# Low halves of two output-weight chunks formed by TensorE and ScalarE instead of TensorE and VectorE, with a new order of all instructions

## The chip, the cores and the metric

One core of one Trainium2 chip. The metric is the device time of one execution in microseconds (us), lower is better. The kernel before took 509.13 us (median of 3 runs, 508.42 to 509.32). One more execution was profiled: it took 508.1 us, and its first to last instruction span 506.3 us.

Engines are named as in the profile: PE is TensorE (PEld its weight loads), DVE is VectorE, ACT is ScalarE, POOL is GpSimd, SP is SyncE, which issues the DMAs.

## What is computed

Banded attention over 8 batches x 8 heads x 576 tokens x 64, then a gated MLP. Inputs q, k, v come as float32, the weights as float64.

```python
scores = where(mask, q @ k.T / 8, -1e9)          # heads 0-3: last 32 keys; heads 4-7: every 32nd key
x = (softmax(scores) @ v) as (B, S, 512)
h = maximum(x @ w_in, 0)                          # w_in 512 x 1024
conv[s] = cw[0]*h[s-1] + cw[1]*h[s] + cw[2]*h[s+1]
out = (h * sigmoid(conv)) @ w_out                 # w_out 1024 x 512
```

## The kernel before, in words

**Split numbers.** The big products keep float32 accuracy with TensorE's faster fp32r type. Each operand is kept as a high half (the value rounded to fp32r) and a low half (what is left), and a product is three fp32r matmuls: high x high, low x high, high x low. `mm1` (L622) makes x @ w_in that way from `wih`, `wil`, `xh`, `xl` (L633); `mm2` (L707) makes the output from `woh`, `wol`, `gh`, `gl` (L721).

**Groups.** The 4608 tokens are worked in 9 groups of 512. A group's `mm1` makes eight 128-row tiles f = 0 to 7; `conv_gate` (L642) takes each through ReLU out of PSUM (ACT, L650), the middle tap (ACT L681, or DVE L684 for some tiles of group 0), two more taps (DVE L690), sigmoid (ACT L694), the gate product (L698, on DVE or POOL) and the split into `gh` (ACT L388) and `gl` (L391, on DVE or POOL). Then `mm2` makes four output tiles. The attention of the next batch (L431 scores, L538 times v, and the softmax between on DVE and ACT) is woven in.

**Weights.** `convert` (L298) takes a chunk of weights from its float64 words: |high word| (ACT L281), a clamp (L283), four integer and float steps on DVE (L285 to L291) that leave a float32 `t` in the word buffer `ws` and a remainder `tail` in `wl`; then ACT rounds `t` to the high half (L355). The low half is t + tail - high. There are eight chunks c = 0 to 7: four of w_in, then w_out's wo0 to wo3 (c = 4 to 7); each low half is made in two pieces. A letter of `SPLIT_W` (L44, by c) says how:

```python
if how == "a":
    def whole(ps=ps, b=b):
        nc.tensor.matmul(ps, eye, half(t, b), start=True, stop=False)      # L368
        nc.tensor.matmul(ps, eyer, half(tail, b), start=False, stop=False) # L369
        nc.tensor.matmul(ps, negr, block(wh, b), start=False, stop=True)   # L370
    ...
    op(A, 0.59, ..., nc.scalar.copy(block(wlo, b), four(ps)))              # L372
else:
    def less(ps=ps, b=b):
        nc.tensor.matmul(ps, eyer, half(tail, b), start=True, stop=False)  # L375
        nc.tensor.matmul(ps, negr, block(wh, b), start=False, stop=True)   # L376
    ...
    op(V, 0.69, ..., nc.vector.tensor_tensor(out=block(wlo, b), in0=four(half(t, b)), in1=four(ps), op=ALU.add))  # L378
```

`eye` is a float32 identity and `t` is float32, so L368 is a full float32 matmul; `eyer` and `negr` are fp32r identities, one of them negated.

**Order.** Every instruction is recorded as an operation with a number (`Plan.op`), and `emit` (L185) issues them in the sequence of the table `ORDER` (L55). Each engine runs its own instructions in that order and waits where an operand or buffer isn't ready. `FILLS` (L139) puts warm-up matmuls (`busy`, L742) that compute nothing ahead of an operation: 9: (18, 1, 18) means 18 of them ahead of operation 9, into PSUM bank 1, the first 18 of them 512 columns wide, the others 256. Bank -1 is the first half of the attention's PSUM tile `r`. The other tables choose engines by letter, p for POOL, v for DVE, a for ACT: `CLAMP` (L283, by chunk), `GATE` and `FIRST_GATE` (L698), `SPLIT_G` and `FIRST_SPLIT_G` (L391), `FIRST_SCALE` (L681 or L684 in group 0).

## Time and profile before

| | |
|---|---|
| median of 3 runs | 509.13 us |
| profiled execution, its time / its span | 508.1 us / 506.3 us |
| PE busy | 495.9 us (98%), 6997 matmuls |
| PE weight loads busy | 401.9 us (79%) |
| DVE busy | 364.8 us (72%) |
| ACT busy | 337.1 us (67%) |
| POOL busy | 138.3 us (27%) |
| DMA | 51.45 MB, mean 102 GB/s |
| warm-up matmuls (L742) | 105 |

Matmuls are pipelined, so the duration of one matmul in a row overlaps the next; what a matmul costs the stream is the distance from its start to the next start. A row of the timeline says how long the engine was idle before it, and what ended that wait.

### The profile page before, as it was taken

The numbers are of one execution on the slowest core, as the hardware profiler recorded it, in microseconds if no ns is written. First come the engines' busy times: TensorE is split into PE (matmuls) and PEld (weight loads), VectorE is DVE, ScalarE is ACT, GpSimd is POOL, SyncE is SP. The second block draws the span as 40 slices with busy tenths as digits, with TensorE's granted clock in tenths as the row PEclk, the third lists the DMA queues.
The fourth block names the chain that finished last, engine by engine and source line by source line (L and its number), as shares of the span: only waits on it lengthen the run. The fifth ranks groups of instructions, "written<-read, shape, count | busy, mean of one in ns | idle before, by whom it ended". The sixth has DMA issues, their size and how long they took to land.

```text
span 506.3 us, 16055 instructions
## 1 busy us (share of the span) xinstructions
PE 495.9 (98%) x6997; PEld 401.9 (79%) x6997; DVE 364.8 (72%) x640; ACT 337.1 (67%) x653; POOL 138.3 (27%) x225
## 2 busy tenths in 40 slices
PE   8899999999999999999999999999999999999997
PEld 4476778887888888887888888888888888888797
DVE  3999998658976786777939896777688846643740
ACT  3877988558846785578648964875588647635741
POOL 1201323223310534055204220414014521442610
PEclk9999999999999999999999999999999999999999
DMA  8776603152142331314151223601442010002002
GB/s 299 286 247 217 241 2 113 66 179 82 34 129 85 112 128 50 138 60 155 38 172 42 65 97 128 197 22 61 131 157 71 1 62 23 1 0 84 0 2 85
DMA packets 17351, 51.45 MB, mean 102 GB/s; under 512 B 2048, under 2 KB 2944, under 8 KB 17280
## 3 DMA queue, kind: packets, MB, share of 16 engines
q1 hardware_dynamic: 17280, 50.41, 29.0%
q8 instruction: 55, 0.90, 0.8%
q14 instruction: 16, 0.13, 0.1%
HBM read 40.97 MB, written 9.44 MB: 100 GB/s over the span
## 4 chain that ended last, share of the span: by engine, by line
PE 77%; ACT 6%; DVE 5%; issue 1%; DMA 1%; POOL 1%; ACTq 0%; DVEq 0%; POOLq 0%
PE m L721 37%; PE m L633 30%; PE r L538 5%; PE r L431 4%; DVE misc L690 2%; ACT misc L681 1%; DMA ws<-in_dram 1%; ACT misc L694 1%; ACT misc L650 1%; ACT gh L388 1%; DVE gl L391 1%; ACT t L467 1%; POOL gl L391 0%; ACT wa L281 0%; DVE misc L698 0%
## 5 line engine op out<-in xcount | busy, mean ns | idle before, releaser
L690 DVE SCALAR_TENSOR_TENSOR misc<-misc,cw 128x512 f32<-128x512 f32 (+25 forms) x256 | 129.3, 549 | 32.4 <-ACT misc L681 31.9
L721 PE MATMUL m<-gh,woh 128*128 128x512 f32 (+2 forms) x320 | 119.9, 375 | 0.7 <-ACT misc L650 0.6
L721 PE MATMUL m<-gl,woh 128*128 128x512 f32 (+2 forms) x320 | 118.0, 369 | 0.2 <-DVE gl L391 0.2
L721 PE MATMUL m<-gh,wol 128*128 128x512 f32 (+2 forms) x320 | 117.8, 368 | 0.0
L633 PE MATMUL m<-xh,wih 128*128 128x512 f32 x288 | 114.1, 396 | 0.0
L633 PE MATMUL m<-xl,wih 128*128 128x512 f32 x288 | 112.4, 390 | 0.2 <-ACT xl L594 0.2
L633 PE MATMUL m<-xh,wil 128*128 128x512 f32 x288 | 112.3, 390 | 0.0
L698 POOL TENSOR_TENSOR misc<-misc 128x512 f32<-128x512 f32 (+1 forms) x40 | 46.4, 1164 | 114.8 <-ACT misc L694 113.9
L721 PEld LDWEIGHTS m<-gh,woh 128*128 128x128 f32 x320 | 60.0, 188 | 11.9 <-ACT misc L650 1.6
L721 PEld LDWEIGHTS m<-gl,woh 128*128 128x128 f32 x320 | 60.1, 188 | 10.9 <-DVE gl L391 0.7
L721 PEld LDWEIGHTS m<-gh,wol 128*128 128x128 f32 x320 | 60.1, 188 | 9.6
L681 ACT ACTIVATE misc<-misc,cw 128x383 f32<-128x383 f32 (+12 forms) x125 | 61.3, 526 | 7.3 <-POOL misc L652 2.8
L694 ACT ACTIVATE misc<-misc 128x512 f32<-128x512 f32 (+1 forms) x72 | 45.3, 632 | 29.5 <-DVE misc L690 29.2
L633 PEld LDWEIGHTS m<-xl,wih 128*128 128x128 f32 x288 | 54.1, 188 | 12.2 <-ACT xl L594 0.7
L633 PEld LDWEIGHTS m<-xh,wih 128*128 128x128 f32 x288 | 54.1, 188 | 11.7 <-ACT misc L650 0.2
L633 PEld LDWEIGHTS m<-xh,wil 128*128 128x128 f32 x288 | 54.1, 188 | 10.8
L391 POOL TENSOR_TENSOR gl<-misc,gh 128x512 fp32r<-128x512 f32 (+1 forms) x38 | 48.1, 1266 | 49.9 <-ACT gh L388 43.6
L388 ACT CAST gh<-misc 128x512 fp32r<-128x512 f32 (+1 forms) x72 | 44.1, 618 | 25.8 <-DVE misc L698 13.9
L650 ACT ACTIVATE misc<-m 128x512 f32<-128x512 f32 x72 | 42.2, 593 | 14.5 <-PE m L633 10.4
L728 ACT COPY misc<-m 128x512 f32<-128x512 f32 (+2 forms) x40 | 21.0, 544 | 35.2 <-PE m L721 35.2
L571 ACT CAST xh<-r 128x576 fp32r<-128x576 f32 (+13 forms) x56 | 23.8, 431 | 28.3 <-DVE t L456 12.6
L652 POOL COPY misc<-carry 128x2 f32<-128x2 f32 x64 | 20.3, 330 | 79.0 <-DVE misc L698 47.4
(77 smaller groups left out, 597.3 us busy)
## 6 DMA issues: line engine op xcount, KB each, us to landing
qk<-in_dram SPq DMA_DIRECT2D x32, 592.0 KB, 5.7
v<-in_dram SPq DMA_DIRECT2D x32, 384.0 KB, 4.4
ws<-in_dram SPq DMA_DIRECT2D x14, 512.0 KB, 4.8
out_dram<-misc SPq DMA_DIRECT2D x28, 256.0 KB, 2.9
misc<-in_dram SPq DMA_DIRECT2D x2, 512.0 KB, 5.2
out_dram<-misc SPq DMA_DIRECT2D x4, 255.5 KB, 2.5
out_dram<-misc SPq DMA_DIRECT2D x3, 256.5 KB, 2.1
more<-in_dram SPq DMA_DIRECT2D x1, 320.0 KB, 7.9
```

Of the source, the lines that this page charges most:

```text
L388: op(A, ta, at, lambda: nc.scalar.copy(hi(), src), [skey], [(k, "h") for k in [key] + over])
L391: lambda: eng.tensor_tensor(out=lo(), in0=src, in1=hi().bitcast(F32), op=ALU.subtract),
L538: nc.tensor.matmul(psV[64 * h:64 * h + 64, o:o + n_], v[W * c:W * c + W, h, j], tt[W * c:W * c + W, 64 * NBLK * h + a:64 * NBLK * h + z], ...
L571: op(A, 0.162 + 0.00083 * (z - a), at + offset[8], lambda hi=hi, src=src: nc.scalar.copy(hi, src), ko, [("xh", hp, x) for x in halves])
L633: nc.tensor.matmul(ps, a[:, c, fs], x[:, c, N * x0:N * x0 + N], start=(n == 0 and m == 0), stop=(n == NC - 1 and m == 2))
L650: op(A, 0.596, at + cg[2], lambda: nc.scalar.activation(out=h[:, 2:N + 2], in_=ps, func=AF.Relu), [kp], [("h", hi)])
L681: op(A, 0.17 + 0.00108 * (z - a), at + cg[3], lambda a=a, z=z: nc.scalar.activation(out=c_[:, a:z], in_=h[:, a + 1:z + 1], func=AF.Copy, s ...
L690: op(V, 0.22 + 0.00103 * (z - a), at + cg[4] + 0.4 * k, lambda k=k, wk=wk, a=a, z=z: nc.vector.scalar_tensor_tensor(out=c_[:, a:z], in0=h[ ...
L694: op(A, 0.63, at + cg[5], lambda: nc.scalar.activation(out=c_[:, :n], in_=c_[:, :n], func=AF.Sigmoid), [kc], [kc], table=1)
L698: op(ge, 0.69 if ge == V else 1.28, at + cg[6], lambda: (nc.vector if ge == V else nc.gpsimd).tensor_tensor(out=c_[:, :n], in0=h[:, 1:n + ...
L721: nc.tensor.matmul(ps, a[:, f, ms], row(y, g, f)[:, tok], start=(f == 0 and n == 0), stop=(f == NF - 1 and n == 2))
L728: op(A, 0.59 if z - a0 == N else 0.38, at + 3 * t + 3, lambda ps=ps, a0=a0, z=z: nc.scalar.copy(o[:, a0:z], ps), [("M", mi)], ko)
```

## The change

It switches chunks c = 5 and c = 7 (wo1 and wo3) from q to a in `SPLIT_W`: for four pieces L375, L376 and L378 go, and L368, L369, L370 and L372 come. It moves the clamp of c = 0, 6 and 7 from POOL to DVE, reassigns gate products and splits between DVE and POOL (p in `SPLIT_G` 35 to 31, in `GATE` 36 to 32; `FIRST_SPLIT_G` and `FIRST_GATE` keep 3 and 4), gives one more middle tap of group 0 to DVE (`FIRST_SCALE`, a 5 to 4), replaces `ORDER` whole, and changes the warm-up matmuls (104 to 99 in the table).

```diff
-SPLIT_W = "qaqqqqqq"
-SPLIT_G = "pvvvppvvppppppvpvppvpvvpppvppvvpvvvpvpppvppvpvppvvvpppvpppvvvvpv"
-GATE = "ppppvvvvpppvvpppppppppvpvpvvvpvvpppvvpvvvvvpppppvpvpvvpvppppvpvv"
-FIRST_SPLIT_G = "vpvvpvpv"
+SPLIT_W = "qaqqqaqa"
+SPLIT_G = "pvvpppvpppvppvvpvvvpppppppvvpvppppvpvpppvvpvvvvpvvvvvvvvpvpvpvvv"
+GATE = "pvvvppvpvpvvvvppppvvpvvpvvpppppvvvvpppppvppvvpppppvvvvvvvppvpvpv"
+FIRST_SPLIT_G = "vvvvpvpp"
-FIRST_GATE = "pvvpvpvp"
-FIRST_SCALE = "aaavvaav"
+FIRST_GATE = "ppvvpvpv"
+FIRST_SCALE = "vavavvaa"
-CLAMP = "pppppppp"
+CLAMP = "vpppppvv"
 ORDER = [
...
-    9: (18, 1, 18), 21: (12, 1, 12), 84: (8, 1, 7), 94: (7, 1, 7), 34: (9, 1, 9), 42: (5, 1, 4), 48: (4, 3, 0), 56: (10, 3, 0), 173: (23, 3, 0), 255:
-    (8, -1, 0),
+    9: (18, 1, 18), 21: (12, 1, 12), 84: (5, 1, 5), 94: (10, 1, 10), 29: (1, 1, 0), 34: (10, 1, 10), 42: (5, 1, 4), 44: (2, 1, 2), 56: (5, 3, 5), 136:
+    (1, 3, 1), 173: (21, 3, 4), 255: (9, 2, 0),
```

Three places show what moves. The first is PE in group 0, where the first piece of wo1's low half is made; `m_92` to `m_95` are the four PSUM banks, `wl_101` is the chunk's remainder, `ws_97` its word buffer. Before:

```order
L633 MATMUL m_92<-xl,wih 128x512
L375 MATMUL m_95<-wl_101,eyer 128x512
L376 MATMUL m_95<-woh,negr 128x512
L633 MATMUL m_93<-xh,wih 128x512
L633 MATMUL m_93<-xh,wil 128x512
```

With the change:

```order
L633 MATMUL m_92<-xl,wih 128x512
L368 MATMUL m_95<-ws_97,consts 128x512
L369 MATMUL m_95<-wl_101,eyer 128x512
L370 MATMUL m_95<-woh,negr 128x512
L633 MATMUL m_93<-xh,wih 128x512
```

One matmul more stands there, L368, at the same place after the same product. wo1's second piece follows two products later; the 8 warm-up matmuls into `r` that stood before L633 in bank `m_92` become 9 into bank `m_94`, and wo3's two pieces stand two and four products behind those before, and both three products behind them with the change.

The second is DVE, just after the last conversion step of wo1 (`wl_101`), one piece of the difference:

```order
 L291 SCALAR_TENSOR_TENSOR wl_101<-ws_97,wa_99 128x1024
+L684 TENSOR_SCALAR misc<-misc,cw 128x512
 L690 SCALAR_TENSOR_TENSOR misc<-misc,cw 128x512 x2
-L378 TENSOR_TENSOR wol<-ws_97,m_95 128x4x128
+L283 TENSOR_SCALAR wa_98<-wa_98 128x1024
 L454 TENSOR_REDUCE mx_80<-r 128x10
 L285 TENSOR_SCALAR wa_98<-wa_98 128x1024
-L378 TENSOR_TENSOR wol<-ws_97,m_95 128x4x128
```

Two adds of wo1 leave DVE; a middle tap and the clamp of wo2 (`wa_98`) come. The 27 DVE rows that end with the first row of this piece stand in both kernels in one order.

The third is ACT over the same stretch, from the rounding of wo1's high half on, one piece of the difference:

```order
 L355 CAST woh<-ws_97 128x8x128
+L281 ACTIVATE wa_98<-ws_96 128x1024
+L372 CAST wol<-m_95 128x4x128
+L650 ACTIVATE misc<-m_93 128x512
 L681 ACTIVATE misc<-misc,cw 128x512
-L281 ACTIVATE wa_98<-ws_96 128x1024
-L694 ACT_TABLE_LOAD
-L694 ACTIVATE misc<-misc 128x512
-L650 ACTIVATE misc<-m_93 128x512
+L694 ACT_TABLE_LOAD
+L694 ACTIVATE misc<-misc 128x512
+L372 CAST wol<-m_95 128x4x128
```

Two copies L372 out of PSUM come into ACT's queue ahead of the exponentials (L467) that follow some ten instructions later.

## Rows read from the trace of the kernel before

**Rows 1.** The page, part 1: busy time, share of the span, instructions.
```profile
PE 495.9 (98%) x6997; PEld 401.9 (79%) x6997; DVE 364.8 (72%) x640; ACT 337.1 (67%) x653; POOL 138.3 (27%) x225
```

**Rows 2.** Windows: length, busy us of PE, PEld, DVE, ACT, POOL; clock, DMA.
```profile
0.00:51.50 51.50, 45.44 (x987) 29.04 (x987) 41.83 (x67) 35.60 (x108) 7.96 (x17) 1.00 0.74 263
51.50:66.20 14.70, 14.66 (x129) 11.70 (x130) 13.81 (x20) 13.79 (x32) 5.40 (x6) 1.00 0.54 192
67.80:231.00 163.20, 163.20 (x2490) 133.87 (x2488) 124.09 (x226) 114.81 (x209) 46.83 (x77) 1.00 0.27 91
231.00:237.00 6.00, 5.88 (x169) 4.44 (x168) 3.60 (x6) 4.55 (x10) 3.67 (x8) 1.00 0.35 108
237.00:479.00 242.00, 242.00 (x3030) 199.35 (x3029) 172.21 (x310) 157.39 (x274) 70.78 (x116) 1.00 0.23 76
479.00:490.00 11.00, 10.20 (x82) 9.64 (x81) 7.69 (x11) 6.45 (x11) 3.64 (x4) 1.00 0.01 2
```

**Rows 3.** The chain that ended last, in order of time: start, us, what.
```profile
90.77 9.74 PE m L721 x42
...
489.70 13.61 PE m L721 x112
```

**Rows 4.** PE's timeline at 24.5 us, the second piece of c = 1.
```profile
24.46 1.06 PE L368 MATMUL m<-ws,consts 128*128 128x512 f32 x2
24.94 0.82 PE L369 MATMUL m<-wl,eyer 128*128 128x512 f32 x1
25.59 0.40 PE L370 MATMUL m<-wih,negr 128*128 128x512 f32 x1
25.83 0.39 PE L742 MATMUL m<-warm 128*128 128x512 bf16 x1
```

**Rows 5.** PE's timeline at 64 us, the second piece of wo2.
```profile
63.97 0.40 PE L375 MATMUL m<-wl,eyer 128*128 128x512 f32 x1
64.20 0.40 PE L376 MATMUL m<-woh,negr 128*128 128x512 f32 x1
64.44 0.39 PE L633 MATMUL m<-xh,wih 128*128 128x512 f32 x1
```

**Rows 6.** PE's timeline at 66 to 68 us.
```profile
66.25 0.39 PE L633 MATMUL m<-xl,wih 128*128 128x512 f32 x1
67.03 1.03 PE L742 MATMUL r<-warm 128*128 128x256 bf16 x8 [0.39 <-ACT t L467]
67.81 0.48 PE L633 MATMUL m<-xh,wih 128*128 128x512 f32 x1
```

**Rows 7.** ACT's timeline, 53 to 67 us.
```profile
53.19 1.15 ACT L281 ACTIVATE wa<-ws 128x1024 f32<-128x1024 f32 x1 [0.72 <-DMA ws<-in_dram]
...
66.54 0.34 ACT L467 ACTIVATE t<-r,mx 128x48 f32<-128x48 f32 x1
...
66.82 0.65 ACT L650 ACTIVATE misc<-m 128x512 f32<-128x512 f32 x1
```

**Rows 8.** Groups by line: names, count, busy us, mean ns, idle before.
```profile
L378 DVE TENSOR_TENSOR wol<-ws,m 128x512 fp32r<-128x512 f32 x8 | 5.4, 683 | 0.6 <-PE m L376 0.5
L372 ACT CAST wil<-m 128x512 fp32r<-128x512 f32 x2 | 1.2, 602 | 0.0
L285 DVE TENSOR_SCALAR wa<-wa 128x1024 int32<-128x1024 int32 (+2 forms) x9 | 5.6, 627 | 7.1 <-POOL wa L283 7.1
L684 DVE TENSOR_SCALAR misc<-misc,cw 128x512 f32<-128x512 f32 x3 | 1.5, 486 | 0.0
L391 DVE TENSOR_TENSOR gl<-misc,gh 128x512 fp32r<-128x512 f32 (+1 forms) x34 | 24.6, 733 | 10.4 <-ACT gh L388 10.3
L512 ACT ACTIVATE t<-t,sm 128x48 f32<-128x48 f32 (+1 forms) x40 | 9.6, 332 | 0.2 <-DVE sm L485 0.2
```

**Rows 9.** Timelines of DVE and POOL in the first 30 us.
```profile
7.84 0.44 DVE L285 TENSOR_SCALAR wa<-wa 128x536 int32<-128x536 int32 x1 [6.84 <-POOL wa L283]
29.41 1.29 DVE L378 TENSOR_TENSOR wil<-ws,m 128x512 fp32r<-128x512 f32 x2 [0.49 <-PE m L376]
...
9.95 0.69 POOL L283 TENSOR_SCALAR wa<-wa 128x512 f32<-128x512 f32 x1 [2.09 <-ACT wa L281]
```

## Prediction

> **What bounds the kernel now.** First the busy shares: PE is busy 98% of the span, no other engine above 72% [rows 1]. A busy matmul may still be one that waits, so next the same by stretch. From 67.8 to 479 us PE has 0.12 us of idle time, all of it between 231 and 237, while DVE and ACT have room: DVE works 124 of 163 us in one of these stretches and 172 of 242 in another; the clock is 1.00, the upper of its two levels, in every stretch [rows 2]. Then the spacing: 42 matmuls of 512 columns take 9.74 us, 0.232 each [rows 3]. That is the pace of the whole middle, so from 67.8 us on the kernel is a queue of PE work, and a microsecond of PE work put in there is a microsecond more. Three places are different. Up to 51.5 us DVE sets the pace: of the 43.7 us after its first real instruction at 7.84 it works some 41.7 (41.83 less a short first fill) [rows 2, 9], and PE's time is filled up with warm-up matmuls. At 66 us PE loses time once: a product starts at 66.25 and would let the next start at 66.48, but that starts at 67.81, so 1.33 us go [rows 6]. From 479 to 490 us it is idle for 0.80 [rows 2], and the chain then ends in 13.61 us of pure PE work [rows 3].

> **The change, part by part.**

> *The four pieces on PE.* The old way costs from 63.97 to 64.44, 0.47 us [rows 5]; the new one from 24.46 to 25.83, 1.37 us [rows 4], since L368 on full float32 data takes about as long as four of the fp32r matmuls. That is 0.90 more for a piece, 3.6 for four. Two pieces (wo1) stand ahead of the wait at 66 us, two (wo3) behind it, where PE never waits: these are 1.80 us on the path. No product leaves PE in exchange.

> [...]

> *The wait at 66 us.* Can it swallow wo1's 1.80? PE arrives 1.80 later, at 66.48 + 1.80 = 68.28. What it waits for there is ACT: ReLU L650 runs at 66.82, behind the exponentials, to free a PSUM bank [rows 6, 7]. Between ACT's conversion step at 53.19 and those exponentials the change adds two copies L372, 0.60 each [rows 8]; the middle tap that moves to DVE (0.49 [rows 8]) lay before a DMA wait of 0.72 [rows 7] and gives nothing back. So the ReLU ends 1.2 later, 67.47 + 1.20 = 68.67. And before the next product stand nine warm-up matmuls in place of eight; eight take 67.03 to 67.81, nine 0.88 [rows 6], so PE is through at 68.28 + 0.88 = 69.16. The ReLU comes before that, the warm-ups decide, and the next product starts 1.35 later than before. Of 1.80 the wait swallows 0.45.

> *What leaves DVE.* Four adds at 0.68, 2.7 us [rows 8]. In come four clamps: for wo2 and wo3 priced by L285's mean, 0.63 each, and two on 536 and 512 columns priced at 0.44 [rows 8, 9], 2.1 in all, and one middle tap at 0.49. DVE's sum stays where it was, within 0.1. The adds that go stood after 52 us, when PE had its products ahead of it, so they were not on the path; had the 2.7 been, the most it could return is the 0.45 swallowed plus the 0.88 still lost at 66 us.

> *The start.* DVE's order is the same over the 27 rows up to wo1's conversion, so the first 51.5 us can move only by what changes before. The first clamp on DVE is waited for, and at about 0.44 it is 0.25 shorter than POOL's 0.69 for that size; the second lies on DVE's own queue, 0.44 more. The wait of 0.49 before L378 [rows 9] may go, since two attention steps now stand ahead of it. Between -0.74 (both gains) and +0.44 (neither) I take 0, near the sum of all three, -0.3. The two ends stay in the range. The DMA queue loads the attention's v somewhat earlier between weight chunks; the weight loads wait for their buffers as before, so nothing is counted.

> *Gates and splits.* Eight more of them on DVE, about 0.73 each [rows 8], 5.8 us over eight groups. DVE has 39 us free in the first long stretch and 70 in the second [rows 2], which hide them; without that cover they cost up to 5.8. Off POOL goes more, which bounds nothing.

> *The new order from 67.8 us on.* Unknown from this trace. Below, it could remove all that is left: 0.12 and 0.80 of idle, -0.9. Above, a buffer or ACT wait of the size of the longest ACT block in front of a copy, ten L512 in 2.4 us (40 of them are busy 9.6 [rows 8]). I take 0, since the nearest row, 242 us of PE work on end without idle time [rows 2], shows that such an order can hold.

> **Sum:** 1.35 + 1.80 = 3.15, call it 3.2: 508.1 + 3.2 = 511.3 against the profiled execution. The median of the three runs is 1.0 above that execution, so in those terms 509.1 + 3.2 = **512.3 us**. A measurement of this kernel can tell 0.2%, 1.0 us, from no change.

> **The rivals.**

> *Half of it is hidden.* If the new order reaches the saturated stretch about 1.3 us sooner, wo1's pieces are free and only wo3's 1.80 remain: 510.9. For: DVE has about 2.0 us of idle time between 7.84 and 51.5 us. Against: its order there hardly changed.

> *Not slower.* DVE's queue is the mechanism: if all that DVE and the waits lose were won back, that is 1.33 at 66 us, 2.0 and 0.25 in the first 51.5, and 0.92 later, 4.5 against 3.6, or 508.2. It decides only if four fifths or more come back together. For: that is what relieving DVE is good for while it is 95% busy. [...] The trace agrees that it is, up to 51.5 us. Against: DVE's sum up to there stays the same.

> *A new wait on ACT.* The first `mm2` product after wo3 needs bank `m_94`, which L372 has to empty; in ACT's queue that stands behind a table load, two sigmoids and two roundings, by my count some 0.4 us ahead of PE, and the copy of the second piece stands behind ten L512 with 0.9 to spare. If ACT runs a microsecond or more late there, PE waits; the price is up to the 2.4 of that block: 514.7.

> *PE has room between its matmuls.* The weight loads are busy 79%, not 98% [rows 1]; if wo3's extra passes slipped in between, 1.35 would stay, 510.5. Against: L368 in the trace takes the time of four fp32r matmuls, no less [rows 4, 5]. [...]

> **How the numbers follow.** The forecast 0.62; half hidden 0.13; not slower 0.07; ACT wait 0.15; room on PE 0.03. The forecast moves by the start's -0.7 to +0.4 and the later order's -0.9 to about as much above, 510.7 to 513.6. The range goes down to 509.9, to take in most of the half-hidden case and of the room on PE, and up to 514.6, most of the ACT wait; not slower and the ends are left out. Faster by over 0.2%: 0.04, half of "not slower" and a little. Within 0.2% (508.1 to 510.1): 0.13, the other half, some of the half-hidden case and the lowest edge of the forecast. Slower: 0.83.

> **What would show it.** Right: L368 four times in group 0 with 1.37 us from piece to next matmul, PE without idle time between about 69 and 480 us, the first product after the warm-ups at about 69.2, and the start of the last pure PE stretch at about 492.9 instead of 489.7. Half hidden: that product at about 67.8. A new wait on ACT: an idle row on PE before L721 at 74 to 80 us ended by ACT's `wol`. The prediction is wrong if the start of the saturated stretch moved by more than half a microsecond, or if idle rows on PE past 237 us add up to more than a microsecond.

## The result, and the profile after the change

The changed kernel took 514.36 us, the median of 4 runs (512.38 to 515.62); the kernel before took 508.95 in the runs beside it. The ratio is 1.0105 with a 95% interval of 1.0089 to 1.0120: 5.4 us slower. The direction of the prediction held, the forecast of 512.3 was 2.1 us too low, and the time lies 0.2 below the upper end of the range. The profiled execution is the slowest of the four, 515.62 us with a span of 513.8; a second trace of the same kernel (a_same below) has a span of 512.2, and both are used.

First the windows of the changed kernel: for each stretch its length, then busy us and count of PE, PEld, DVE, ACT and POOL, the granted clock of PE, the DMA share and GB/s.

```profile
0.00:51.50 51.50, 46.44 (x929) 28.01 (x930) 41.86 (x68) 34.79 (x107) 7.80 (x15) 1.00 0.75 262
51.50:68.00 16.50, 16.50 (x208) 13.02 (x193) 16.25 (x23) 14.89 (x30) 5.12 (x5) 1.00 0.57 199
68.00:80.00 12.00, 11.76 (x52) 8.59 (x51) 10.86 (x20) 11.91 (x36) 1.14 (x2) 1.00 0.00 1
80.00:237.00 157.00, 156.56 (x2488) 128.53 (x2489) 119.38 (x214) 108.47 (x193) 41.76 (x73) 1.00 0.30 99
237.00:479.00 242.00, 240.99 (x3165) 198.22 (x3143) 172.33 (x310) 151.67 (x268) 63.49 (x111) 1.00 0.22 75
479.00:490.00 11.00, 9.01 (x46) 7.75 (x46) 8.09 (x11) 7.64 (x13) 5.91 (x7) 0.90 0.00 1
```

Against [rows 2] three things differ. PE has small losses in the middle, 0.44 and 1.01 us, where it had almost none. From 479 to 490 us it is idle for 1.99 us in place of 0.80. And there the granted clock, which was 1.00 in every stretch, is 0.90.

The four pieces cost what was priced. PE's timeline at wo3, which answers to [rows 4, 5]:

```profile
72.04 1.06 PE L368 MATMUL m<-ws,consts 128*128 128x512 f32 x2
72.52 0.81 PE L369 MATMUL m<-wl,eyer 128*128 128x512 f32 x1
73.17 0.40 PE L370 MATMUL m<-woh,negr 128*128 128x512 f32 x1
73.40 1.06 PE L368 MATMUL m<-ws,consts 128*128 128x512 f32 x2
```

From piece to piece it is 73.40 - 72.04 = 1.36 us; forecast was 1.37. The place of [rows 6]:

```profile
68.20 0.39 PE L633 MATMUL m<-xl,wih 128*128 128x512 f32 x1
68.43 1.16 PE L742 MATMUL m<-warm 128*128 128x256 bf16 x9
69.83 0.50 PE L633 MATMUL m<-xh,wih 128*128 128x512 f32 x1 [0.24 <-ACT misc L650]
```

The product behind the warm-ups starts at 69.83, 2.02 later than before, where 1.35 was forecast. ScalarE's first copy and the ReLU for that product, from its timeline:

```profile
55.39 0.59 ACT L372 CAST wol<-m 128x512 fp32r<-128x512 f32 x1 [1.30 <-PE m L370]
...
69.13 0.65 ACT L650 ACTIVATE misc<-m 128x512 f32<-128x512 f32 x1
```

And this is the end of the work, in PE's timeline of the last token group:

```profile
484.19 0.39 PE L633 MATMUL m<-xl,wih 128*128 128x512 f32 x1
486.57 0.39 PE L721 MATMUL m<-gh,woh 128*128 128x256 f32 x1 [1.99 <-ACT misc L650]
486.79 0.28 PE L721 MATMUL m<-gh,wol 128*128 128x256 f32 x1
486.91 0.29 PE L721 MATMUL m<-gl,woh 128*128 128x256 f32 x1
...
487.77 0.42 PE L721 MATMUL m<-gh,woh 128*128 128x258 f32 x1
487.99 0.42 PE L721 MATMUL m<-gh,wol 128*128 128x258 f32 x1
```

PE waits 1.99 us for ScalarE's ReLU. The first products after it follow each other by 0.12 us, those from 487.77 on by 0.22: the same work at half the clock, which was granted at 1.00 from 479 to 487 us and at 0.50 from 488 to 491.

To compare whole traces, the products L633 and L721 are counted (1824 in every kernel), and the start of one is compared with that of the same number in the kernel before. All experiments stand in this table; the four right-hand columns are that delay in us, in the one profiled execution of each. Their heads give the number of the product and its start in the kernel before.

| kernel | ratio to before, interval | 1st (34.9 us) | 101st (75.3) | 1401st (426.2) | last (503.0) |
|---|---|---|---|---|---|
| changed kernel, first trace | 1.0105 [1.0089, 1.0120] | +0.53 | +3.86 | +5.28 | +7.54 |
| a_same | 1.0109 [1.0086, 1.0131] | -0.11 | +3.41 | +3.41 | +5.92 |
| a_q | 1.0187 [1.0174, 1.0200] | +1.20 | +9.11 | +10.32 | +9.43 |
| b_a | 1.0106 [1.0094, 1.0118] | +0.33 | +5.67 | +5.66 | +5.67 |
| a_tail | 1.0087 [1.0071, 1.0103] | +0.50 | +3.69 | +4.09 | +4.07 |
| a_table | 1.0085 [1.0071, 1.0100] | +0.02 | +3.37 | +3.59 | +3.87 |
| a_fill | 1.0080 [1.0061, 1.0100] | +1.50 | +5.58 | +5.48 | +6.12 |
| a_both | 1.0075 [1.0055, 1.0095] | +1.51 | +4.79 | +4.14 | +4.11 |
| b_pe | 1.0287 [1.0267, 1.0307] | +0.58 | +3.68 | +15.30 | +15.28 |
| b_pe2 | 1.0054 [1.0039, 1.0069] | +0.23 | +3.42 | +3.30 | +3.28 |
| b_shift | 1.0301 [1.0274, 1.0329] | +0.48 | +0.87 | +15.93 | +15.90 |
| b_plus | 1.0021 [1.0009, 1.0032] | +0.01 | +0.74 | +0.51 | +0.55 |

### The profile page after: what moved, and what is told of

The parts are those of the page before. It is cut to its first block, busy times and chain, and to the rows that moved or that the text cites. A ratio compares the mean times of both kernels' runs of the same rounds, so it can differ in the third digit from the quotient of the medians.

```text
span 513.8 us, 16045 instructions
## 1 busy us (share of the span) xinstructions
PE 502.1 (98%) x7000; PEld 404.7 (79%) x7000; DVE 373.4 (73%) x649; ACT 335.4 (65%) x654; POOL 126.9 (25%) x213
## 4 chain that ended last, share of the span: by engine, by line
PE 81%; DVE 4%; ACT 3%; issue 1%; DMA 1%; POOL 1%; POOLq 0%; SPq 0%; ACTq 0%
PE m L721 39%; PE m L633 31%; PE r L538 5%; PE r L431 4%; DVE misc L690 2%; DMA out_dram<-misc 1%; ACT misc L681 1%; ACT t L467 1%; DVE ws L287 0%; ACT misc L694 0%; PE m L368 0%; ACT misc L650 0%; POOL misc L652 0%; DVE wa L289 0%; ACT L467 0%
## 5 line engine op out<-in xcount | busy, mean ns | idle before, releaser
L690 DVE SCALAR_TENSOR_TENSOR misc<-misc,cw 128x512 f32<-128x512 f32 (+24 forms) x256 | 133.3, 564 | 39.3 <-ACT misc L681 38.4
L721 PE MATMUL m<-gh,woh 128*128 128x512 f32 (+2 forms) x320 | 120.4, 376 | 2.0 <-ACT misc L650 2.0
L721 PE MATMUL m<-gh,wol 128*128 128x512 f32 (+2 forms) x320 | 118.5, 370 | 0.0
L721 PE MATMUL m<-gl,woh 128*128 128x512 f32 (+2 forms) x320 | 118.5, 370 | 0.0
L633 PE MATMUL m<-xh,wih 128*128 128x512 f32 x288 | 113.9, 396 | 0.2 <-ACT misc L650 0.2
L633 PE MATMUL m<-xl,wih 128*128 128x512 f32 x288 | 112.2, 390 | 0.4 <-issue 0.4
L633 PE MATMUL m<-xh,wil 128*128 128x512 f32 x288 | 112.3, 390 | 0.0
L698 POOL TENSOR_TENSOR misc<-misc 128x512 f32<-128x512 f32 (+1 forms) x36 | 41.8, 1162 | 119.7 <-ACT misc L694 113.1
L721 PEld LDWEIGHTS m<-gh,woh 128*128 128x128 f32 x320 | 60.9, 190 | 13.0 <-ACT misc L650 2.8
L721 PEld LDWEIGHTS m<-gl,woh 128*128 128x128 f32 x320 | 60.8, 190 | 10.2
L721 PEld LDWEIGHTS m<-gh,wol 128*128 128x128 f32 x320 | 60.9, 190 | 9.6
L681 ACT ACTIVATE misc<-misc,cw 128x257 f32<-128x257 f32 (+12 forms) x124 | 60.5, 524 | 8.9 <-POOL misc L652 4.7
L633 PEld LDWEIGHTS m<-xh,wih 128*128 128x128 f32 x288 | 54.0, 188 | 12.4 <-issue 0.6
L633 PEld LDWEIGHTS m<-xl,wih 128*128 128x128 f32 x288 | 54.1, 188 | 11.5
L633 PEld LDWEIGHTS m<-xh,wil 128*128 128x128 f32 x288 | 54.1, 188 | 10.8
L650 ACT ACTIVATE misc<-m 128x512 f32<-128x512 f32 x72 | 42.6, 594 | 18.8 <-PE m L633 16.1
L391 POOL TENSOR_TENSOR gl<-misc,gh 128x512 fp32r<-128x512 f32 (+1 forms) x34 | 42.1, 1239 | 49.4 <-ACT gh L388 49.1
L728 ACT COPY misc<-m 128x512 f32<-128x512 f32 (+2 forms) x40 | 20.7, 548 | 34.9 <-PE m L721 34.5
L652 POOL COPY misc<-carry 128x2 f32<-128x2 f32 x64 | 18.0, 295 | 101.2 <-DMA out_dram<-misc 63.3
## 6 DMA issues: line engine op xcount, KB each, us to landing
ws<-in_dram SPq DMA_DIRECT2D x14, 512.0 KB, 4.4
misc<-in_dram SPq DMA_DIRECT2D x2, 512.0 KB, 5.0
```

Of the source, the lines that this page charges most:

```text
L391: lambda: eng.tensor_tensor(out=lo(), in0=src, in1=hi().bitcast(F32), op=ALU.subtract),
L633: nc.tensor.matmul(ps, a[:, c, fs], x[:, c, N * x0:N * x0 + N], start=(n == 0 and m == 0), stop=(n == NC - 1 and m == 2))
L650: op(A, 0.596, at + cg[2], lambda: nc.scalar.activation(out=h[:, 2:N + 2], in_=ps, func=AF.Relu), [kp], [("h", hi)])
L681: op(A, 0.17 + 0.00108 * (z - a), at + cg[3], lambda a=a, z=z: nc.scalar.activation(out=c_[:, a:z], in_=h[:, a + 1:z + 1], func=AF.Copy, s ...
L690: op(V, 0.22 + 0.00103 * (z - a), at + cg[4] + 0.4 * k, lambda k=k, wk=wk, a=a, z=z: nc.vector.scalar_tensor_tensor(out=c_[:, a:z], in0=h[ ...
L698: op(ge, 0.69 if ge == V else 1.28, at + cg[6], lambda: (nc.vector if ge == V else nc.gpsimd).tensor_tensor(out=c_[:, :n], in0=h[:, 1:n + ...
```

## Experiments

The theory after the first trace had three parts. The products cost the 3.15 us of the sum, on their own. The new order costs a later start, and a wait in the last group. That wait makes the clock fall. The rival was that one cause carries all: the products and their sequel, or the order.

**One part undone, one part alone.** a_q takes the changed kernel and gives the four pieces back to `less` and VectorE; two neighbours in the order change places, since one now reads a bank that the other writes.

```diff
-SPLIT_W = "qaqqqaqa"
+SPLIT_W = "qaqqqqqq"
-    214, 282, 215, 179,
+    214, 215, 282, 179,
```

> The changed kernel with its order and letters, but the four pieces of the second and the fourth chunk of w_out go back to `less` on TensorE and the sum on VectorE. Theory (the extra products and the new order each cost on their own): the four pieces on the path were summed at 1.35 + 1.80 = 3.15 us, so 514.4 - 3.15 = 511.2; the late first activation, the 1.99 us wait near 484.6 and the half clock after it stay. Rival 1 (all of the difference comes from the products on TensorE, and the wait and the clock at the end are their sequel): 509.0, and no wait over 1 us near 481. Rival 2 (the products are hidden, the order carries all): 514.4.

It took 518.07 us, 3.7 more than with the pieces. Every theory named here was wrong. The waits of PE from 49 to 80 us (for whom; sum, times, longest) and the windows with the clock:

```profile
PE m L633 <- ACT misc L650: 3.5, 2, 2.2
PE m L375 <- DVE wl L291: 1.2, 1, 1.2
```

```profile
60.00:63.00 3.00, 1.74 (x7) 0.86 (x5) 2.93 (x5) 2.86 (x5) 1.91 (x3) 1.00 0.00 0
63.00:68.00 5.00, 3.76 (x10) 2.94 (x10) 4.79 (x8) 0.70 (x2) 1.28 (x1) 0.66 0.41 133
```

VectorE gets its four adds back, 2.7 us [rows 8], in an order that has no place for them: it works 2.93 of 3 us and 4.79 of 5. PE waits 1.2 us for VectorE and 3.5 for ScalarE's ReLU, and the granted clock of one stretch is 0.66. What holds the ReLU is only in part VectorE: ahead of the first of the two, ScalarE had waited 1.14 us for VectorE's L287, ahead of the second 4.81 for a load of weights.

b_a is the other half: the kernel before, with the pieces moved and nothing else.

```diff
-SPLIT_W = "qaqqqqqq"
+SPLIT_W = "qaqqqaqa"
```

> The kernel before with its own order and letters, and only the word for the second and the fourth chunk of w_out changed, so that their four pieces go by `whole` and a copy on ScalarE. Theory: +3.15 us as summed, 512.1, with the start of the saturated stretch 1.35 us later and no new wait after 237 us; clock 1.000. Rival 1 (the products carry all): 514.4. Rival 2 (products hidden, order carries all): 509.0. If ScalarE, with two more copies in an order that was not made for them, holds TensorE between 66 and 80 us, up to 513.3.

513.77 us, 5.3 more than before, 0.5 above the bound that was given for a late ScalarE. All of it is there at 75 us (5.67 in the trace, of which 0.33 stood at the first product). The four pieces are 4 x 0.89 = 3.6 of it, and two ScalarE waits 0.9. PE waits from 49 to 80 us:

```profile
PE m L633 <- ACT misc L650: 0.9, 2, 0.5
...
PE r L742 <- ACT t L467: 0.5, 1, 0.5
```

So neither time gives a price. The pieces alone cost 5.3 us, the order with its other letters alone 9.6, both together 5.4: order and split fit only together, and a half of them without the other shows how badly it fits.

**The end.** a_tail follows the changed order up to the first product of the eighth token group, and then takes the rest in the order of the kernel before, with its letters for the last two groups. The diff shows the ends of the letter tables and the first numbers of the order that differ; ... stands for the rest.

```diff
-SPLIT_G = "...vvvvvvvvpvpvpvvv"
+SPLIT_G = "...vvvpppvpppvvvvpv"
-GATE = "...ppvvvvvvvppvpvpv"
+GATE = "...vpvpvvpvppppvpvv"
 ORDER = [
...
-    ... 1764, 1784, 1787, 1785, 1786, 1732, 1733, 1734, 1735, 1737, 1742, 1743, 1765, 1766, 1744, 1788, 1789, ...
+    ... 1764, 1784, 1665, 1787, 1788, 1732, 1733, 1737, 1734, 1735, 1742, 1743, 1744, 1789, 1765, 1790, ...
```

> The changed kernel up to the first product of the eighth token group; from there the rest of the instructions in the order of the kernel before, and the engines of the gates and low halves of the last two groups as before. Theory (the order of the last two groups makes the 1.99 us wait, and the wait makes the clock fall): the wait falls to the 0.58 and 0.28 us of the kernel before, the clock stays 1.000; 1.99 - 0.86 = 1.1 and 1.7 us less, 514.4 - 2.8 = 511.6. Rival 1 (the end waits because all before it is late; order has no part in it): 514.4 with the same wait. Rival 2 (the wait goes, the clock falls all the same): 513.3.

The wait and the fall of the clock are gone: from the 1401st product to the last the delay goes from 4.09 to 4.07, where the changed kernel adds 2.3 and 2.5. PE's waits after 69 us, as in the kernel before but for `issue` (0.6, and 0.3 at L538) and the 0.2 us at 70 us:

```profile
PE m L721 <- ACT misc L650: 0.6, 1, 0.6
PE m L633 <- issue: 0.6, 1, 0.6
...
PE m L721 <- DVE gl L391: 0.2, 1, 0.2
```

The median, 512.86, is 1.3 above what was expected; its interval overlaps that of the changed kernel, so it is the traces that show this step. What differs there is also in the traces. Both orders run the output products of the eighth group ahead of nearly all input products of the ninth. But in the changed kernel the chain of waits goes through an output transfer (462.32 to 466.86), out of a buffer that the ninth group's gates need; GpSimd's copy into it waited for that:

```profile
467.00 0.19 POOL L652 COPY misc<-carry 128x2 f32<-128x2 f32 x1 [19.78 <-DMA out_dram<-misc]
```

In a_same the chain has such a transfer, too (4.76 us from 460.45); in the kernel before and in a_tail it has none. a_tail takes back the order and the letters of these groups together, so which of the two does more is not shown.

a_fill leaves the wait and puts work into it.

```diff
-    (1, 3, 1), 173: (21, 3, 4), 255: (9, 2, 0),
+    (1, 3, 1), 173: (21, 3, 4), 255: (9, 2, 0), 2086: (17, -1, 0),
```

> The changed kernel with 17 narrow warm-up products into the free first half of r, ahead of the product that waits 1.99 us in the last group. Theory (the idle TensorE makes the clock fall a little later): the wait becomes busy time and its length stays, the granted clock stays 1.00 from 479 us to the last product, up to 1.7 us less than the same kernel without them. Rival 1 (the clock falls for another reason): as without them, clock 0.997. Rival 2 (the products come when TensorE is not idle and are paid): up to 1.8 us more.

512.57 us, against 514.33 of the changed kernel in the same group of runs: 1.8 less, as expected. The window of the end and PE's timeline in it:

```profile
479.00:490.00 11.00, 11.00 (x74) 9.69 (x73) 8.08 (x11) 7.73 (x14) 5.92 (x7) 1.00 0.01 2
```

```profile
484.62 2.03 PE L742 MATMUL r<-warm 128*128 128x256 bf16 x17
```

The waiting time is as long as before, the clock stays at 1.00, and the delay grows by 0.64 us behind the 1401st product in place of 2.3 and 2.5. The intervals of the two kernels overlap, so here, too, the traces carry the argument. All its runs but one have a clock of 1.000 over the whole span; of the changed kernel's ten in both groups three have, so the fall doesn't come in every execution. That at this place it comes with the idle PE, and is worth over a microsecond, is shown.

**The start.** a_table moves the copy that makes `negr` ahead of the first Abs again.

```diff
-    0, 1, 76, 2, 74, 86, 87, 88, 89, 90, 93, 5, 19, ...
+    0, 1, 76, 2, 74, 5, 86, 87, 88, 89, 90, 93, 19, ...
```

> The changed kernel with one instruction moved: the ScalarE copy that makes negr stands ahead of the first Abs again, so that the table load is put ahead of it. Theory (the load of the activation table ran for 1.28 us behind the wait for the first weights): the table load stands near 0.7 us, the first Abs at 6.4 instead of 7.13 us, the saturated stretch starts up to 1.0 us earlier; 513.4 to 513.9. Rival (the first stretch is set by VectorE's and GpSimd's chains, or by loads): the table load moves and the saturated stretch starts within 0.2 us of 51.14; 514.4.

ScalarE's first rows in the changed kernel, and with the copy moved:

```profile
5.84 1.28 ACT L281 ACT_TABLE_LOAD   x1 [5.84 <-DMA misc<-in_dram]
7.13 0.69 ACT L281 ACTIVATE wa<-misc 128x536 f32<-128x536 f32 x1
```

```profile
0.73 1.28 ACT L750 ACT_TABLE_LOAD   x1 [0.73 <-PEq L850]
5.12 0.31 ACT L750 ACTIVATE negr<-consts 128x128 fp32r<-128x128 f32 x1 [3.10 <-DMA consts<-in_dram]
6.50 0.68 ACT L281 ACTIVATE wa<-misc 128x536 f32<-128x536 f32 x1 [1.07 <-DMA misc<-in_dram]
```

512.52 us, under the 513.4 to 513.9 that were expected. The table load (ACT_TABLE_LOAD in the rows) stands at 0.73 in place of behind the wait for the first weights. The first product comes 0.5 us earlier than in the first trace, and the saturated stretch starts at 50.68 in place of 51.14 us. But in a_same, without the edit, the first product comes as early (-0.11 in the table), and that stretch starts at 50.74. By ratio the kernel is about 1.1 us faster, with overlapping intervals; how much of that is the table can't be told from it, since the wait at the end, too, is shorter in this trace (1.23 us) and the clock stays at 1.00 there. The weights land at 4.7 to 6.5 us from execution to execution, and in the traces of a_fill and a_both the first product is 1.5 us late with the first Abs at 7.26 and at 5.14, so other loads count too.

a_both has the edits of a_table and a_tail in one.

> The moved negr copy and the order of the last two groups from the kernel before, both at once. Theory (they are two separate losses): 3.4 us over the kernel before at 75 us, as with the first alone, up to 0.9 us of issue idle time after that, nothing at the end: 3.4 to 4.3 us over before, 512.0 to 512.8. Rival (what the start gives is lost at the end): as the better of the two alone, 512.5 to 512.9, with a wait at the end.

512.50 us; the delay at the last product, 4.11, lies between the 3.4 and 4.3 that were expected, with no wait of 2 us at the end. By median it is not clearly better than either edit alone: the runs of all these kernels scatter by 2.3 to 3.4 us, those of the kernel before by 1.4 to 2.9, and this trace has a late start, 1.51.

**The base again.** a_same is the changed kernel without an edit.

> The changed kernel once more, unchanged, as the base of this group and for a second trace of it. Theory (the wait at the end follows from the order, idle time on TensorE put down to issue comes anew in each execution): a wait of 1 to 2 us on ScalarE's L650 near 484 us again, some 0.5 to 1.5 us of idle time by issue past 80 us at places that partly differ from the first trace; 1.010 of the kernel before. Rival (both were accidents of one execution): no wait over 0.9 us at the end.

514.33 us; PE's waits after 69 us in its trace, and, second, in the first trace of that kernel:

```profile
PE m L721 <- ACT misc L650: 2.2, 1, 2.2
PE m L633 <- ACT misc L650: 0.2, 1, 0.2
```

```profile
PE m L721 <- ACT misc L650: 2.0, 1, 2.0
PE r L538 <- issue: 1.1, 2, 0.7
PE m L633 <- issue: 0.4, 1, 0.4
PE m L633 <- ACT misc L650: 0.2, 1, 0.2
```

The wait at the end belongs to the kernel; the 1.5 us by `issue` came in one execution and not in the other, where 0.5 to 1.5 were expected.

**TensorE's time alone.** b_pe keeps everything of the kernel before and adds only PE time, as much as `whole` has over `less`.

```diff
-    (8, -1, 0),
+    (8, -1, 0), 212: (8, 3, 0), 214: (8, 3, 0), 290: (8, 2, 0), 292: (8, 3, 0),
```

> The kernel before with 8 narrow warm-up products ahead of each of the four `less` of the second and the fourth chunk of w_out, into the bank that `less` then clears: TensorE gets 4 times 0.86 = 3.4 us more, and no other engine gets or loses anything. Theory (TensorE's time there is on the path): 3.4 less the 0.4 us that the warm-ups and the wait at 66 to 68 us swallow = 3.0, 511.5. Rival 1 (TensorE has room there, what cost the time in the word-only run was ScalarE): 508.5 to 509.5. Rival 2 (later arrival makes VectorE late, too, since its four sums wait for `less`): over 512.5.

523.44 us, 15 more. That is beyond 512.5 as the second rival had it, but not by its cause: no wait for VectorE of over 0.3 us stands in the trace after 69 us. At 75 us the delay is 3.68, of which 0.58 was there at the first product: 3.1, as priced. The rest comes later. PE's waits after 69 us, and two rows of its timeline:

```profile
PE r L538 <- issue: 6.9, 5, 2.7
PE m L633 <- ACT misc L650: 2.0, 1, 2.0
PE m L721 <- ACT misc L650: 0.6, 1, 0.6
```

```profile
105.06 0.97 PE L538 MATMUL r<-tt,v 32*64 32x2 f32 x75
108.73 0.31 PE L538 MATMUL r<-tt,v 32*64 32x32 f32 x5 [2.71 <-issue]
```

Inside a burst of 80 small products of the attention, after 75 of them, PE stops for 2.71 us and waits for nothing that the profile shows. Four other bursts stop in the same way, a few products before their end. The last of the 32 added products ran 30 us earlier, but the 32 move every later instruction along PE's stream. The page's table of DMA queues has `q8 instruction: 55` packets with 0.90 MB, some 16 KB each, which come all through the span. The new theory: PE's instructions come in such blocks, and where a block ends in a burst of short instructions, the next isn't there yet. Two runs test it.

b_shift adds no work. It splits 32 wide warm-ups of the first 14 us into two narrow ones each.

```diff
-    9: (18, 1, 18), 21: (12, 1, 12), 84: (8, 1, 7), ...
+    9: (36, 1, 0), 21: (24, 1, 0), 84: (10, 1, 5), ...
```

> The kernel before with 32 of its wide warm-up products before 14 us each replaced by two narrow ones: the same columns, 32 products more in TensorE's stream, all work after 14 us as before, and every later instruction as far back in the stream as in the last run past 75 us. Theory (TensorE idled in that run where a block of its instructions came too late, and where the block ends fall in a burst of small products decides it): idle time by issue at L538 near 105, 240, 307, 332 and 400 us, 4 to 9 us in all, 512 to 518. Rival (the idle time came from the later arrival of the work, or from the products in the banks): 508 to 509.5 and no idle time by issue.

The theory of blocks holds, but its size was too small: 524.24 us, 15.9 us for nothing but 32 more products in the first microseconds. PE's waits after 69 us, its timeline at the second of the stops, and the DMA traffic from 241 to 245 us (in 40 slices, then the packets by queue):

```profile
PE r L538 <- issue: 8.8, 5, 2.6
PE m L633 <- ACT gh L388: 1.7, 1, 1.7
```

```profile
240.80 0.87 PE L538 MATMUL r<-tt,v 32*64 32x36 f32 x62
243.90 0.41 PE L538 MATMUL r<-tt,v 32*64 32x32 f32 x6 [2.23 <-issue]
```

```profile
GB/s 0 0 0 0 0 164 0 0 0 0 0 0 0 0 0 0 0 0 0 0 0 0 0 0 0 0 0 0 0 0 0 0 0 0 0 0 0 0 0 0
DMA packets 1, 0.02 MB, mean 4 GB/s; under 512 B 0, under 2 KB 0, under 8 KB 0
q8 instruction: 1, 0.02, 1.5%
```

The five stops came as forecast, 1 to 7 us later each: 105.87, 243.90, 313.56, 336.54 and 404.75. Around the second one the only packet that moves on any queue is one block of instructions, from about 241.5 to 242.5 us, while PE stands still until 243.90. Idle rows make up 11.1 us of the 15; much of the rest is the clock, whose mean is 0.98 from 80 to 150 and 0.97 from 240 to 300 us.

b_pe2 has the columns of b_pe in half as many products, and takes 16 products out of earlier warm-ups, so that past 75 us the stream is as long as before.

```diff
-    ... 48: (4, 3, 0), 56: (10, 3, 0), 173: (23, 3, 0), 255: (8, -1, 0),
+    ... 48: (4, 3, 0), 56: (5, 3, 5), 173: (12, 3, 11), 255: (8, -1, 0),
+    212: (4, 3, 4), 214: (4, 3, 4), 290: (4, 2, 4), 292: (4, 3, 4),
```

> As b_pe, but with 4 wide warm-up products ahead of each `less` in place of 8 narrow ones, and 16 fewer products in two warm-ups before 52 us (the same columns there in half the products): TensorE gets the same 3.4 us more, and past 75 us its stream is as long as in the kernel before. Theory (blocks of instructions): no idle time by issue past 80 us; the 3.1 us that b_pe had at 75 us stay to the end, 511.6. Rival (the extra columns set off the idle time): 518 to 523 as b_pe.

511.28 us, 2.9 more than before, no `issue` row after 69 us, a delay of 3.42 at 75 us (0.23 of it from the start) and 3.28 at the end. Both halves are shown: of the 3.4 us of extra PE time 3.2 stay on the path, and the 12 us between b_pe and b_pe2 come with the place in the stream. That this place is a block's end the traces show by counting. Over all of PE's instructions (matmuls, weight loads and some 60 others), all 35 stops by `issue` of over 0.05 us in the thirteen traces stand 193 or 194 instructions behind a multiple of 256, whatever the kernel (51.54 us in the kernel before and 47.55, 136.01, 264.28 and 359.49 in the first trace of the changed one are five of them), and PE goes on 1.2 to 1.6 us after the packet of a block is through.

**Towards a faster kernel.** b_plus attacks the two waits of the kernel before. It sets the bank's last products and the ReLU ahead of the exponentials (with the gate that frees its buffer), drops the 8 warm-ups there and splits 8 early ones to keep the stream's length; and a tiny copy lets the table load run first. In the tables ... stands for what is the same in both.

```diff
-    0, 1, 76, 74, 2, 5, 19, 18, 86, 87, ...
+    0, 1, 76, 74, 2, 19, 18, 86, 5, 87, ...
-    216, 217, 183, 247, 250, 158, 159, 304, 143, 184, 298, 248, 194, 229, 230, 249, 251, 231, 253, 218, 219, 232, 160, 150,
-    252, 282, 283, 299, 196, 284, 182, 285, 161, 220, 255, ...
+    216, 217, 218, 219, 183, 247, 250, 158, 159, 304, 143, 184, 298, 248, 194, 249, 160, 161, 251, 229, 253, 230, 231, 232,
+    150, 252, 282, 283, 220, 299, 196, 284, 182, 285, 255, ...
-    ... 21: (12, 1, 12), ... 255:
-    (8, -1, 0),
+    ... 21: (20, 1, 4), ...
-        op(V, 0.1, -20, lambda: nc.vector.memset(warm_, 0.0), (), ["warm"])
+        def first_():
+            nc.vector.memset(warm_, 0.0)
+            nc.scalar.copy(negr[:, 0:2], warm_[:, 0:2])
+        op(V, 0.1, -20, first_, (), ["warm"])
```

> The kernel before with its two largest waits before 70 us attacked: two products of the fifth feature block and the step that reads its bank go ahead of the exponentials, so that TensorE needn't wait at 66.5 to 67.8 us (the 8 warm-ups there go, 8 more stand in the first microseconds); and a tiny copy on ScalarE at the very start lets the table load run early, with the first Abs ahead of negr. Theory (both waits are on the path): 1.33 us at the first, up to 0.5 us at the second: 507.0. Rival (VectorE, busy 11.3 of 12 us from 68 to 80, then holds TensorE there): the wait comes back before 80 us, 508.3.

509.41 us, 1.0 slower: the rival by its mechanism, 1.1 above its time. The wait at 66 us is gone and comes back as this one (lines are one lower here, L374 is L375 of before), behind a VectorE that has no gap in front of it and runs this step 0.9 us later than before (67.68):

```profile
69.86 0.50 PE L374 MATMUL m<-wl,eyer 128*128 128x512 f32 x1 [1.63 <-DVE wl L290]
```

```profile
68.46 0.17 DVE L479 TENSOR_SCALAR sm<-sm 128x10 f32<-128x10 f32 x1
68.58 1.22 DVE L290 SCALAR_TENSOR_TENSOR wl<-ws,wa 128x1024 fp32r<-128x1024 uint32 x1
```

Its first Abs ran at 4.68 us, 1.7 earlier than before, and the first product no earlier (+0.01). No kernel here beats the one before.

## Why the prediction was right, and where it was wrong

**The four pieces on PE: right.** 0.90 a piece was forecast, 1.36 in place of 0.47 measured. That such time is on the path is what b_pe2 shows: 2.9 us by median, 2.0 to 3.5 by its interval, for 3.4 added.

**The wait at 66 us: the step was wrong, the sum held by luck.** The wait was to swallow 0.45 us of wo1's 1.80. It swallowed nothing: the last product ahead of the warm-ups runs 1.95 us later (68.20 in place of 66.25), the first behind them 2.02, and 1.40 us go there in place of 1.33, where 0.88 was forecast. The prediction had the ReLU end at 68.67 and let the warm-ups decide. The ReLU ended at 69.78, and PE waited 0.24 for it (0.23 in a_same). The sum had added the time of two copies to ScalarE's queue; that the first of them waits for its product on PE, 1.30 us, it left out. Even so the delay grows by 3.33 and 3.52 from the 1st product to the 101st in the two traces of the changed kernel, and by 3.35, 3.19 and 3.28 in a_table, a_tail and a_both; the sum said 1.35 + 1.80 = 3.15. The four pieces are 4 x 0.89 = 3.56 of that, and 0.1 to 0.4 comes back ahead of the wait. The new order is what brings it there: the old one, given the same pieces, lost 5.3 (b_a). The prediction had no step for that; it took for granted that an order made anew would fit.

**What leaves DVE: right that it returns nothing by itself.** In b_a the four adds are gone from VectorE, and nothing came back. b_plus shows that VectorE holds PE at 70 us as soon as another wait goes, and a_q that the new order has no room for the four adds: without their leaving it doesn't hold.

**The start, taken as 0: a term was missing, and its size is open.** VectorE's order was compared, ScalarE's wasn't: there an Abs that waits for its weights came first, and the table load went behind that wait. In the first trace and in a_tail the first Abs runs at 7.1 us in place of 6.41, and the first product is 0.5 late; in a_same, where the weights landed at 5.18 in place of 5.84, neither is late by more than 0.1. a_table doesn't settle what the load costs. The prediction's own test, a saturated stretch that starts over half a microsecond later, came true: 51.14 against 50.10. But it did so in a_same and a_table, too (50.74 and 50.68), without a late first product; what makes that part is not shown.

**The new order from 67.8 us on, taken as 0: the step that failed.** From the 1401st product to the last the delay grows by 2.3 and 2.5 us. 1.99 and 2.2 of wait stand in place of 0.6 and 0.2, 1.2 and 1.4 net, and the other 1.1 is the clock: from 487.77 on 15 products follow each other by 0.214 in place of 0.12 [rows 3], 1.4 us, of which 0.3 comes back elsewhere in that stretch. "242 us of PE work on end without idle time" was the wrong row to go by: it tells of groups in the middle, each with a next group to draw work from. The last group has none, and that stretch of the trace had idle time already, 0.80 us [rows 2]. The bound, +2.4 from a ScalarE block, was nearly right in size, by chance, since it was meant for another place; and it left out the fall of the clock behind such a wait (0.50 after 1.99 us here), which no row before could show. The other sign of error that the prediction named, idle rows of over a microsecond past 237 us, came true.

**The rivals.** The ScalarE wait at 74 to 80 us did not come: no idle row stands there, and the 0.24 at 69.83 is all. In b_a PE waits 0.41 for ScalarE at 78.51, but for a ReLU (L650) and not for `wol`. Half hidden and not slower are out by the growth of 3.3. Room on PE is out by the 1.36 us from piece to piece, and by b_pe2.

**The sum again:** 3.3 for the pieces in the new order, 0 to 0.5 for the start, 2.4 for the end, 0 to 1.5 by `issue`: 5.7 to 7.7, against 5.92 and 7.54 in the two traces and 5.4 and 5.8 by the medians. So the time fell into the range for another reason than the one that set its upper end, the ScalarE wait at 74 to 80 us; without what happened in the last group it would have been near the forecast. What remains open is the scatter of the start by the landing of the loads, and the length of the stops by `issue`: past 200 us the two traces of the changed kernel have them at the same two places of the stream, 0.36 and 0.65 us in the one, under 0.1 each in the other.

## What to carry to other kernels

Where an order was found as a whole, taking back one part of the change prices the misfit, not the part; add the suspected cost to the unchanged kernel as dummy work on that engine alone, and keep the instruction stream's length. In a forecast of a new order read first what has least cover: the last groups, where nothing follows to fill a wait, and the first instructions of every engine, not only of the busiest. When PE idles by `issue` in bursts of small products, shift the stream by some tens of instructions before looking for another cause: here 32 products more, without more columns, made 15.9 us.

## What was not expected of the hardware

**The clock.** The granted clock fell to 0.50 after PE had idled for 1.99 us (from 487.7 to 491) and for 2.2 us (in a_same). The traces of the kernel before and of the changed one show it at 1.00 or at 0.50; a figure between is the mean of a stretch. The clock stayed at 1.00 when 17 narrow matmuls filled the same time (a_fill). With the slower products such a wait of 2 us cost 3.4 here. The length of a wait alone doesn't decide it. In b_pe the clock stayed at 1.00 after PE had stood still for 2.71 us (before 108.73) and for 2.0 (between 130 and 190): the 512-column products take 0.39 to 0.40 us each by the mean in both stretches. It fell there after a stop of 1.36 us (before 311.95), with 0.63 us for each of the six products from 312.83 on. In a_q it fell with waits of 1.26 and 1.24 us: PE is idle for that long from 60 to 63 and from 63 to 68 us, and the clock's mean in the second stretch is 0.66.

**The table load.** The activation table load of 1.28 us took over the wait of the activation that it belongs to and ran behind it, from 5.84 to 7.13 us. With the copy that makes `negr` in front it ran at 0.73, though that copy itself waited for a transfer (until 5.12 in a_table). Why the one load waits and the other doesn't is not shown.
